# Attention feeding a SwiGLU block on one core: the first tiles' probabilities scaled by ScalarE and GpSimd ahead of plain transposes, and one threshold instruction for both heads

## The chip, the cores and the metric

The kernel runs on one core of one Trainium2 chip. The metric is the device time of one execution in microseconds (us), as the median over several executions. Five engines run their own instruction queues in order: PE (TensorE, matrix products and transposes), DVE (VectorE), ACT (ScalarE), POOL (GpSimd) and SP (SyncE, which here issues DMAs). An instruction starts when the one before it on its engine has been issued and the semaphores it waits for have arrived.

## The reference, cut to what matters

```python
# attention: q, k, v are (8, 8, 576, 64) float32
scores = scale * np.matmul(q, k.transpose(0, 1, 3, 2))
thresh = np.max(scores, axis=-1, keepdims=True) - tau
scores = np.where(scores >= thresh, scores, -1000000000.0)
scores = scores - np.max(scores, axis=-1, keepdims=True)
attn = np.exp(scores)
attn = attn / (np.sum(attn, axis=-1, keepdims=True) + 1e-09)
attn_out = np.matmul(attn, v)
# bridge: (B, H, S, D) -> x of (4608, 512); then, with weights that arrive as 64-bit floats
g = x @ w_gate
out = (g / (1 + np.exp(-g)) * (x @ w_val)) @ w_out
```

Each row of `scores` is cut at its own maximum minus `tau`, exponentiated, and divided by its own sum. What the change touches is how that division reaches the product with `v`, for a part of batch 0.

## The kernel before, in words

The batch is the outer loop. Batch 0 is handled by generators written out in an order by hand (`scores`, `flip_steps`, `attend_tile`, the `split_weights` family and `fill`). Batches 1 to 7 are handled by a planner (`Plan`), which orders jobs by cost; it is not touched by the change.

In batch 0 the heads are taken in four pairs, and a tile is 128 queries of one pair, so that two heads go through each step together. The first eight tiles are queries 0 to 255 of the four pairs, two tiles for each pair (`t < TA`, with `TA = 2`). The twelve tiles after them are the other queries of the same pairs (t = 2, 3 and 4; t = 4 has 64 queries, and its two heads share one tile of 128 rows). Here tiles are numbered in the order in which they run: 0 to 7 are the first eight, 8 to 19 the twelve after them.

One tile goes through these steps, with the line numbers of the kernel before:

- PE makes the scores of both heads into two PSUM tiles `sc` (L438). These PSUM tiles are two in number, so the scores of tile k+1 can start only when the masking of tile k has read them.
- DVE takes the negated row maximum `nm` of each head (L455).
- ACT computes the threshold `th` (L458) and the exponential into `p` (L459), for each head.
- DVE masks `p` against the threshold and sums its rows in the same instruction (L462). Two small instructions turn the sums into the reciprocal `ri` (L464, L465).
- The division. For tiles 8 and later, ACT multiplies the `p` of head 0 by `ri` (L472), and POOL does it for head 1 (L470). For tiles 0 to 7 `p` stays as it is, and ACT makes for each head a 128 x 128 diagonal matrix with `ri` on it (L478, from the identity).
- One tile later PE turns `p` round, so that keys lie on partitions: `flip_steps`. For tiles 8 and later these are transposes against the identity (L506); for tiles 0 to 7 they are matrix products of `p` with the diagonal (L508), which turn and divide at once. The 64 keys left over go through L512 or L514 into a bank `end`. ACT copies the results out of PSUM (L515, L522).
- One more tile later PE multiplies with `v` (L539, L541), and ACT copies the result into `x` (L544).

So while tile k is scored, tile k-1 is flipped and tile k-2 is attended: PE's order within tile k's slot is scores of k, product with `v` of k-2, flip of k-1.

Between these steps the same engines rebuild the FFN's weights, which come as 64-bit floats, one piece of 128 x 768 in each slot from tile 1 on. SP fetches a piece (L282), ACT splits it in two (L298, L299), POOL clamps the upper part (L291), one slot later DVE shifts it (L318), and one more later DVE joins the sign (L324) and POOL adds the lower part (L334). POOL also multiplies the queries by the softmax scale (L371) when their DMAs have landed.

The order on POOL matters. Within the first four segments (tiles 0 to 7) `early_slots[0]` is true, and `split_weights` issues the clamp at once, ahead of what the tile's generator issues next:

```python
            if n or x:
                split_weights()
                fetch_weights(2)
            next(go)
            clamp_split()
            add_lower(1)
```

Here `next(go)` runs the part of `scores` that holds L462 to L472. The scaling of the queries is called after it (`scales.popleft()()`), and the addition of the lower part belongs to `join_weights()` of the next slot. After tile 7 an extra attend of the tile just flipped comes, and then the first gate products (L555), before the scores of tile 9.

Of the kernel before, what the change touches and what calls it, by code (L numbers as in the profile page):

```python
# [13 lines left out]
AF = mybir.ActivationFunctionType  # L14
ALU = mybir.AluOpType
# [12 lines left out]
class Plan:  # L28
# [68 lines left out]
    def pe(self, took, fn, *deps):  # L97
        self.force(*deps)
        for d in deps:
            if d is not None:  # L100
                self.t = max(self.t, (d.end if isinstance(d, Job) else d) + self.HOP)
        self.run(self.t)
        fn()
        self.t += took
        return self.t + self.PIPE
# [7 lines left out]
def kernel(  # L113
# [11 lines left out]
    nc = tc.nc  # L125
    P = 128
# [21 lines left out]
    TA = 2  # L148
# [13 lines left out]
    cut = const.tile([P, 1], F32, name="cut")  # L162
# [48 lines left out]
    def room(n):  # L211
        nonlocal at
        at += n
        return pall[:, at - n:at]
# [3 lines left out]
    pbufs = deque(room(2 * S).rearrange("p (h s) -> p h s", h=2) for _ in range(2))  # L218
    ident = room(P)
    make_identity(nc, ident)  # L220
    dbufs = deque(room(2 * P).rearrange("p (h q) -> p h q", h=2) for _ in range(2))
    ones = room(TC)
    nc.vector.memset(ones, 1.0)
    pTbufs = deque(rall[:, 2 * x * S:2 * (x + 1) * S] for x in range(2))
# [198 lines left out]
    def turned(t):  # L423
        return TA <= t < NT

    def statistics(*names):
        return [stp.tile([P, 2 * NU3, 2] if x == "mx" else [P, 2 * NU3], F32, name=x) for x in names]

    def scores(seg, t):
        qT, kT = seg["qT"], seg["kT"]  # L430
        q0 = t * P - seg["q0"]
        if t < NT:
            pss = [ps_s.tile([P, 2, 512], F32, name="sc") for _ in range(2)]
            for h, hs in enumerate(heads):
                cut_ = D if turned(t) and h == 1 else 0
                for n, lo, to in [(0, 0, D), (0, D, SH), (1, 0, SH)] if cut_ else [(0, 0, SH), (1, 0, SH)]:
                    at_ = (n * SH + lo - cut_) % S
                    nc.tensor.matmul(pss[h][:, n, lo:to], qT[hs, q0:q0 + P], kT[hs, at_:at_ + to - lo],  # L438
                                     start=True, stop=True)
        else:  # L440
            pss = [ps_s.tile([P, 2, 512], F32, name="sc")]
            for n, h in ((0, 0), (1, 1), (1, 0), (0, 1)):
                hs = heads[h]
                nc.tensor.matmul(pss[0][hs, n, 0:SH], qT[hs, q0:q0 + D], kT[hs, n * SH:(n + 1) * SH],
                                 start=True, stop=True)
        nm, th, ri, tot = statistics("nm", "th", "ri", "tot")
        sm = sums[0]
        sums.rotate(1)
        m = len(pss)
        scs = [ps[:, :, 0:SH] for ps in pss]  # L450
        both = pbufs[0].rearrange("p h s -> p (h s)")[:, KM:KM + P]
        ps = [pbufs[0][:, x, :].rearrange("p (n s) -> p n s", n=2) for x in range(m)]
        pbufs.rotate(1)
        for x in range(m):
            nc.vector.tensor_reduce(out=nm[:, x:x + 1], in_=scs[x], axis=AX.XY, op=ALU.max, negate=True)  # L455
        yield
        for x in range(m):
            nc.scalar.activation(th[:, x:x + 1], nm[:, x:x + 1], AF.Identity, bias=cut, scale=-1.0)  # L458
            nc.scalar.activation(ps[x], scs[x], AF.Exp, bias=nm[:, x:x + 1])  # L459
        yield  # L460
        for x in range(m):
            nc.vector.scalar_tensor_tensor(out=ps[x], in0=scs[x], scalar=th[:, x:x + 1], in1=ps[x],  # L462
                                           op0=ALU.is_ge, op1=ALU.mult, accum_out=sm[:, x, 0:1])
        nc.vector.tensor_reduce(out=tot[:, 0:m], in_=sm[:, 0:m, 0:3:2], axis=AX.X, op=ALU.add)  # L464
        nc.vector.reciprocal(out=ri[:, 0:m], in_=tot[:, 0:m])  # L465
        units = [ident] * m
        if t >= TA:
            for x in range(m):
                if x % 2:
                    nc.gpsimd.tensor_scalar(out=ps[x], in0=ps[x], scalar1=ri[:, x:x + 1], scalar2=None, op0=ALU.mult)  # L470
                else:
                    nc.scalar.activation(ps[x], ps[x], AF.Copy, scale=ri[:, x:x + 1])  # L472
        yield
        if t < TA:
            units = [dbufs[0][:, x, :] for x in range(m)]
            dbufs.rotate(1)
            for x in range(m):
                nc.scalar.activation(units[x], ident, AF.Copy, scale=ri[:, x:x + 1])  # L478
        unflipped.append((seg, t, both, [(p.rearrange("p n s -> p (n s)"), unit) for p, unit in zip(ps, units)]))
        yield  # L480

# [44 lines left out]
    def attend_tile(copy=lambda xa, fn: (fn(), give_back(xa))):  # L526
        if not unattended:
            return
        if not xts:
            for u, lo in enumerate((0, 2 * XW)):  # L530
                xts["full", u] = xall[:, lo:lo + XW].rearrange("p (c n) -> p c n", c=NCC)
            xts["last", 0] = xlast
        seg, t, pT, pT2 = unattended.popleft()
        vr, vr2 = seg["v"]
        n = pT2.shape[1]
        xa = bank("xa")
        for kt in range(KT):
            for h in range(2):
                nc.tensor.matmul(xa[h * D:(h + 1) * D, 0:n], vr[:, h, kt, :], pT[:, h, kt, :],  # L539
                                 start=(kt == 0), stop=False)  # L540
        nc.tensor.matmul(xa[:, 0:n], vr2, pT2, start=False, stop=True)  # L541
        u, lo = divmod(t * P, TC)
        to = xts[("last", 0) if t == NT else ("full", u)][:, seg["i"], lo:lo + n]
        copy(xa, lambda: nc.scalar.copy(to, xa[:, 0:n]))  # L544
# [155 lines left out]
    for n, seg in enumerate(segs[:2 * NP]):  # L700
        early_slots[0] = n < NP
        if n >= NP:
            seg["v"] = segs[seg["i"]]["v"]
        for x, t in enumerate(seg["tiles"]):
            go = scores(seg, t)
            next(go)
            join_weights()
# [1246 lines left out]
    for s, (n, x) in enumerate((n, x) for n in range(len(halved)) for x in range(NU3)):  # L1954
        seg = halved[n]
        i, t = seg["i"], seg["tiles"][x]
# [11 lines left out]
        elif s == 1:  # L1968
            box = []
            m = pe(1.0, lambda: attend_tile(lambda *y: box.extend(y)))  # L1970
# [93 lines left out]
```

## Time and profile before

| | |
|---|---|
| time, median of 3 executions | 1373.08 us (1371.66 to 1374.05) |
| span of the profiled execution, first to last instruction | 1369.2 us |
| median less span | 3.88 us |
| the profiled execution's own time | not listed apart from its span |
| PE busy over the span | 1351.0 us (99%) |
| DVE, ACT, POOL busy over the span | 1070.9 (78%), 875.5 (64%), 719.9 (53%) us |
| granted TensorE clock | 1.000 over the span |
| tiles 0 to 7 (L508 products) | within the first 56 us |
| tiles 8 to 19 | about 50 to 130 us |

The page of a profile gives busy time per engine, the chain of work that ended last, and groups of instructions by source line. The timeline lists instructions in order: start, duration, engine, line, what is written and read, and in brackets the idle time of the engine just before it with what ended it. Consecutive like instructions are merged ("x16"), with one duration for all. An instruction's duration is longer than the distance to the next on the same engine where the two overlap.

### The profile page before, as it was taken

Reading aid. Unit: us, or ns where it says so; the run is one execution under the profiler, and the core shown is the slowest. Engines: PE = TensorE matmul, PEld = TensorE weight load, DVE = VectorE, ACT = ScalarE, POOL = GpSimd, SP = SyncE. Lnnn points to the kernel's source line nnn. Section 1 sums busy time; section 2 is a strip of 40 time slices with the busy share of each in tenths; the row PEclk is TensorE's granted clock in tenths of the full one; section 3 lists DMA queues with packets and bytes.
Section 4 is the critical chain, followed back from the end, with each engine's and each line's share of the span. In section 5 each row is a group of like instructions: output and inputs, shape, how many; then the busy total and the mean of one; then the engine's idle time right before and its main releaser. Section 6 shows DMA issues by size and latency. Waiting matters only on the chain.

```text
span 1369.2 us, 39187 instructions
## 1 busy us (share of the span) xinstructions
PE 1351.0 (99%) x15590; PEld 1116.1 (82%) x15590; DVE 1070.9 (78%) x2815; ACT 875.5 (64%) x2277; POOL 719.9 (53%) x665
## 2 busy tenths in 40 slices
PE   8999999999999999999999999999999999999998
PEld 7777787778788788877887888877887788999998
DVE  7878888887887777777778777777777776787786
ACT  6888776666756766677776766776767764330330
POOL 2688598663564669434973387427943593000000
PEclk9999999999999999999999999999999999999999
DMA  8752424545525540654154513553165403524411
GB/s 177 200 185 90 82 60 133 146 121 156 151 52 155 144 98 27 181 159 117 37 171 128 150 36 128 144 144 87 36 192 144 113 19 143 162 78 146 151 66 32
DMA packets 208294, 162.32 MB, mean 119 GB/s; under 512 B 166128, under 2 KB 180464, under 8 KB 202736
## 3 DMA queue, kind: packets, MB, share of 16 engines
q1 hardware_dynamic: 203920, 158.86, 41.3%
q8 instruction: 124, 2.03, 0.6%
q10 hardware_dynamic: 4192, 0.95, 0.3%
q14 instruction: 58, 0.48, 0.1%
HBM read 138.28 MB, written 21.50 MB: 117 GB/s over the span
## 4 chain that ended last, share of the span: by engine, by line
PE 90%; DVE 3%; DMA 2%; POOL 2%; SPq 1%; issue 1%; ACT 1%; ACTq 0%; DVEq 0%; POOLq 0%
PE pb L993 18%; PE pa L993 12%; PE px L1473 12%; PE sc L1705 10%; PE pe L993 9%; PE xa L1802 9%; PE po L1269 5%; PE py L1482 5%; PE sc L1154 2%; PE pg L1200 2%; PE pv L1200 2%; PE pe L1154 1%; SPq L367 1%; DMA wo<-in_moe_w_val_dram 1%; PE sc L1473 1%
## 5 line engine op out<-in xcount | busy, mean ns | idle before, releaser
L1753 DVE SCALAR_TENSOR_TENSOR pall<-sc,th,pall 128x288 f32<-128x288 f32 x504 | 244.0, 514 | 65.1 <-ACT pall L1751 50.7
L993 PE MATMUL pb<-xall,big 128*128 128x256 f32 x1152 | 273.5, 380 | 0.0
L1751 ACT ACTIVATE pall<-sc,nm 128x288 f32<-128x288 f32 x504 | 232.2, 498 | 34.1 <-DVE pall L1753 33.8
L993 PEld LDWEIGHTS pb<-xall,big 128*128 128x128 f32 x1152 | 216.4, 190 | 31.0 <-issue 2.2
L1781 DVE STREAM_TRANSPOSE pall<-pall 128x576 f32<-128x576 f32 x252 | 189.7, 765 | 58.2 <-ACT pall L1779 41.4
L1779 ACT ACTIVATE pall<-pall,ri 128x288 f32<-128x288 f32 x415 | 189.8, 529 | 26.3 <-DVE ri L1767 25.8
L846 POOL TENSOR_TENSOR hall<-hall,tmp 128x512 f32<-128x512 f32 x80 | 102.3, 1279 | 159.3 <-DVE hall L1046 141.9
L993 PE MATMUL pa<-xall,big 128*128 128x256 f32 x768 | 183.4, 382 | 0.0
L993 PEld LDWEIGHTS pa<-xall,big 128*128 128x128 f32 x768 | 143.0, 190 | 22.2 <-issue 2.7
L1705 PE MATMUL sc<-kT,qT 64*32 64x144 f32 (+1 forms) x5376 | 150.0, 345 | 2.9 <-DVE pall L1753 1.7
L1726 DVE TENSOR_REDUCE mx<-sc 128x2 f32<-128x576 f32 x168 | 124.8, 743 | 28.6 <-PE sc L1705 28.1
L1705 PEld LDWEIGHTS sc<-kT,qT 64*32 64x32 f32 x5376 | 97.8, 106 | 56.9 <-issue 21.0
L993 PE MATMUL pe<-xall,big 128*128 128x256 f32 x576 | 137.2, 381 | 0.4 <-issue 0.4
L1802 PE MATMUL xa<-pall,vall 64*32 64x288 f32 x4032 | 133.0, 404 | 0.9 <-DVE hall L1046 0.8
L1776 POOL TENSOR_SCALAR pall<-pall,ri 128x288 f32<-128x288 f32 x89 | 88.9, 1010 | 67.0 <-DVE ri L1767 63.8
L993 PEld LDWEIGHTS pe<-xall,big 128*128 128x128 f32 x576 | 108.5, 190 | 17.3 <-issue 2.8
L1802 PEld LDWEIGHTS xa<-pall,vall 64*32 64x32 f32 x4032 | 76.5, 107 | 50.6 <-issue 7.4
L1761 ACT COPY sums<-sums 32x6 f32<-32x6 f32 x336 | 66.8, 199 | 45.6 <-DVE pall L1753 41.1
L1045 ACT ACTIVATE vall<-tmp 128x512 f32<-128x512 f32 x96 | 60.2, 630 | 24.6 <-DVE tmp L1058 9.0
L1482 PE MATMUL py<-wo,hall 128*128 128x256 f32 x336 | 74.8, 379 | 0.0
L1728 DVE TENSOR_REDUCE mx<-sc 128x1 f32<-128x288 f32 x168 | 74.8, 445 | 0.0
L846 POOL TENSOR_TENSOR tmp<-tmp 128x512 f32<-128x512 f32 x36 | 45.9, 1276 | 53.4 <-ACT tmp L1068 53.4
(258 smaller groups left out, 2481.3 us busy)
## 6 DMA issues: line engine op xcount, KB each, us to landing
big<-sums_hbm SPq DMA_DIRECT2D x42, 1024.0 KB, 5.4
big<-sums_hbm SPq DMA_DIRECT2D x48, 768.0 KB, 4.7
vall<-in_v_dram SPq DMA_DIRECT2D x112, 144.0 KB, 3.0
out_dram<-big SPq DMA_DIRECT2D x32, 256.0 KB, 3.0
qT<-in_q_dram SPq DMA_DIRECT2D x112, 72.0 KB, 4.8
kT<-in_k_dram SPq DMA_DIRECT2D x112, 72.0 KB, 3.0
wo<-in_moe_w_gate_dram SPq DMA_DIRECT2D x16, 384.0 KB, 4.1
wo<-in_moe_w_val_dram SPq DMA_DIRECT2D x16, 384.0 KB, 4.8
```

The lines of the kernel that those rows point to most:

```text
L846: return lambda: nc.gpsimd.tensor_tensor(out=out, in0=a, in1=b, op=op)
L993: nc.tensor.matmul(ps[:, i], w[:, k_, i * P:(i + 1) * P], x[:, k_, :], start=first and i == k_ == 0, stop=True, skip_group_check=True)
L1473: nc.tensor.matmul(ps, a[:, f, :], ws[n][:, f, :], start=bank_ not in begun, stop=True, skip_group_check=True)
L1482: nc.tensor.matmul(ps(), a[:, f, i * P:(i + 1) * P], operands[o][:, f, :], start=first and f == 0, stop=True, skip_group_check=True)
L1705: nc.tensor.matmul(pss[h][(slice(g * G, (g + 1) * G), *part)], qT[hs, col:col + G], kT[hs, c * SH + keys[0]:c * SH + keys[1]], start=True, ...
L1726: rs.append(job("DVE", 0.72, lambda n=n, tile_=tile_: nc.vector.tensor_reduce(out=mx[:, n:n + 2, 0], in_=tile_[:, :, 0:SH], axis=AX.X, op= ...
L1751: ej = job("ACT", 0.42, lambda x=x, n=n: nc.scalar.activation(ps[x], scs[x], AF.Exp, bias=nm[:, n:n + 1]), ej, *((masks[h, 0], masks[h, 1] ...
L1753: masks[x] = job("DVE", 0.45, lambda x=x, n=n: nc.vector.scalar_tensor_tensor(out=ps[x], in0=scs[x], scalar=th[:, n:n + 1], in1=ps[x], op0 ...
L1776: scaled.append(job("POOL", 1.02, lambda x=x, n=n: nc.gpsimd.tensor_scalar(out=x, in0=x, scalar1=ri[:, n:n + 1], scalar2=None, op0=ALU.mul ...
L1779: scaled.append(job("ACT", 0.46, lambda x=x, n=n: nc.scalar.activation(x, x, AF.Copy, scale=ri[:, n:n + 1]), rj, rank=rank))
L1781: seg["turned"].append(job("DVE", 0.72, lambda both=both: nc.vector.transpose(out=both, in_=both), *scaled, rank=rank))
L1802: nc.tensor.matmul(holds[a].ap()[x * G:(x + 1) * G, 0:SH].rearrange("d (i q) -> d i q", q=G), vr[rs, h, j, ds], p[rs, h, :, j, :], start=( ...
```

## The change

Two things change in `scores`. The threshold is computed once for both heads (one instruction on 128 x 2 instead of two on 128 x 1), and it stands behind the exponential of head 0 instead of ahead of it; this holds for all twenty tiles of batch 0. For tiles 0 to 7 the diagonal matrices go, and `p` is multiplied by `ri` as in the later tiles: head 0 by ACT, head 1 by POOL. `flip_steps` is the same code, but its `unit` is now always the identity, so that tiles 0 to 7 take the branch of L506 (transposes) instead of L508. The products of the left-over keys (L512) stay, with the identity in place of the diagonal. The buffers of the diagonals are not allocated any more.

```diff
-    dbufs = deque(room(2 * P).rearrange("p (h q) -> p h q", h=2) for _ in range(2))
...
         for x in range(m):
-            nc.scalar.activation(th[:, x:x + 1], nm[:, x:x + 1], AF.Identity, bias=cut, scale=-1.0)
             nc.scalar.activation(ps[x], scs[x], AF.Exp, bias=nm[:, x:x + 1])
+            if x == 0:
+                nc.scalar.activation(th[:, 0:m], nm[:, 0:m], AF.Identity, bias=cut, scale=-1.0)
...
         units = [ident] * m
-        if t >= TA:
-            for x in range(m):
-                if x % 2:
-                    nc.gpsimd.tensor_scalar(out=ps[x], in0=ps[x], scalar1=ri[:, x:x + 1], scalar2=None, op0=ALU.mult)
-                else:
-                    nc.scalar.activation(ps[x], ps[x], AF.Copy, scale=ri[:, x:x + 1])
+        for x in range(m):
+            if x % 2:
+                nc.gpsimd.tensor_scalar(out=ps[x], in0=ps[x], scalar1=ri[:, x:x + 1], scalar2=None, op0=ALU.mult)
+            else:
+                nc.scalar.activation(ps[x], ps[x], AF.Copy, scale=ri[:, x:x + 1])
         yield
-        if t < TA:
-            units = [dbufs[0][:, x, :] for x in range(m)]
-            dbufs.rotate(1)
-            for x in range(m):
-                nc.scalar.activation(units[x], ident, AF.Copy, scale=ri[:, x:x + 1])
```

In the built order of the changed program, PE, DVE and SP hold the same instructions in the same order as before, apart from the transposes in place of the products. ACT's scaling of `p` stands where the two diagonals stood. On POOL, from tile 1 to tile 7, the new multiplication stands behind that tile's clamp, and ahead of the scaling of queries and of the addition of the next slot.

## The prediction

> **What bounds the stage now.** I read the page's chain first, then the busy time by stretches, then the chain of waits from 36 to 64 us, then the timeline from 8 to 90 us.
>
> ```profile
> PE 90%; DVE 3%; DMA 2%; POOL 2%; SPq 1%; issue 1%; ACT 1%; ACTq 0%; DVEq 0%; POOLq 0%
> ```
>
> Over the whole kernel PE sets the time, but the change lies in batch 0, and a stage has its own limits. The busy times by stretches (stretch, its length, then PE, PEld, DVE, ACT, POOL):
>
> ```profile
> 28.00:42.00 14.00, 12.84 (x115) 10.07 (x112) 13.39 (x26) 12.26 (x27) 10.84 (x9) 1.00 0.74 185
> 42.00:56.00 14.00, 13.48 (x116) 10.97 (x116) 12.47 (x27) 13.79 (x34) 10.85 (x8) 1.00 0.83 172
> ```
>
> ACT, DVE and PE are all nearly full, and POOL has some 3.2 us free in each 14. The chain of waits (start, length, what):
>
> ```profile
> 34.24 5.73 DMA wo<-in_moe_w_val_dram
> ...
> 41.86 0.30 ACT pall L478
> 42.16 0.04 issue
> 42.21 2.05 PE tp L508 x16
> ...
> 47.73 1.80 PE tp L508 x16
> ...
> 55.41 0.62 ACT big L515
> 56.03 0.04 issue
> 56.08 1.09 PE xa L539 x14
> 57.16 0.42 PE xa L541 x2
> 57.58 2.59 PE pg L555 x12
> 60.17 1.29 PE sc L438 x9
> ```
>
> A weight piece that lands at 39.97 resets the stage: ACT had stood idle 1.37 us for it. Then flips and ACT copies lead to the scores of tile 9 at 60.1 us. From there the chain goes on over DVE, POOL and PE with no DMA until 140, so I take a shift of tile 9's scores as a shift of the end, and 3.88 us (1373.08 - 1369.2) around the span as unchanged.
>
> **PE's part.** The flip of a tile was 16 rows of L508 in 1.95 us (at 24.64, 30.15); eight transposes L506 took 1.05 us (at 81.31). That removes 0.9 us a tile, 7.2 in eight tiles. What it is worth depends on who else is full.
>
> **ACT's part.** A threshold holds ACT 0.20 us (L458 at 9.57, the exponential at 9.77); one of two goes. The two diagonals held it 0.59 us (41.76 to the threshold at 42.35); the scaling of `p` holds it 0.66 us (L472 at 66.62, next at 67.28). Net -0.13 us a tile. ACT has 0.21 us idle in all from 41.76 to 53.5, so even with PE relieved this part alone gives about -0.13 x 3 = -0.4 us after the reset at 40.05, and PE's 0.9 goes into waiting for ACT. The new order of threshold and exponential costs nothing: before, the exponential ended 0.92 us after the threshold's start; now it ends at 0.72, and the threshold, from 0.62 on, takes 0.30 and ends at 0.92 too, which is when the masking can start. The wait for the second maximum (0.66 us later) lies under the exponential (0.72). In tiles 8 to 19 I take 0: masking there stands behind the second maximum and L324 on DVE.
>
> **POOL's part.** Eight multiplications of 1.87 us (L470 at 56.49, 65.79) are new, 15 us. Tiles 0 to 2 have room: POOL was idle 6.17, 3.52 and 4.57 us. Then, from the timeline:
>
> ```profile
> 28.75 0.93 POOL L371 TENSOR_SCALAR hall<-hall,scl 128x256 f32<-128x256 f32 x1 [4.57 <-DMA hall<-in_q_dram]
> 29.64 2.60 POOL L334 TENSOR_TENSOR big<-big,extra 128x768 uint32<-128x768 uint32 x1
> ...
> 30.15 1.95 PE L508 MATMUL tp<-pall 128*128 128x128 f32 x16
> ...
> 32.21 0.83 POOL L291 TENSOR_SCALAR big<-big 128x768 f32<-128x768 f32 x1
> 32.40 1.42 PE L438 MATMUL sc<-pall,qT 64*128 64x288 f32 x8
> 33.02 1.24 POOL L371 TENSOR_SCALAR hall<-hall,scl 128x320 f32<-128x320 f32 x1
> 34.23 1.81 POOL L334 TENSOR_TENSOR big<-big 128x768 uint32<-128x768 uint32 x1
> ```
>
> POOL waits for queries until 28.75, adds, and clamps tile 3's piece at 32.21. None of that moves, since SP's train of DMA issues is the same. The multiplication for tile 3 is queued behind this clamp, though `ri` of tile 3 was there at 27.9. Its flip, which ran from 30.15, now waits. Queued behind the flip on PE are its left-over products and the scores of tile 5; on ACT, the copies out of PSUM, and behind these tile 4's split, scaling and tile 5's exponential. Step by step (hops of 0.04 us):
>
> - Tile 3. Multiplication 33.04 + 1.87 = 34.9. Four transposes hold PE 0.5, the left-over products 0.37: scores of tile 5 at 35.8 (before 32.40, +3.4). ACT's last copies end about 36.2, so tile 4's L298 starts there (before 32.83, +3.4).
> - Tile 4. POOL: 34.9 + L371 1.08 + L334 1.81 = 37.8, clamp 0.83 = 38.6, multiplication 1.87 = 40.5. Transposes and copies 1.4: tile 5's L298 at 41.9 to 42.4 (before 40.05, +1.9 to +2.3; the upper value where L324 at 38.4 holds POOL's start back 0.5). The 1.37 us for which ACT used to wait for its DMA has paid for the difference.
> - Tile 5. A new ring: L298 0.93, clamp 0.83, multiplication 1.87, four transposes to their end 0.66, copy 0.59, last copy's start 0.16, five hops 0.2: 5.24 us. L298 stood 5.18 apart before (40.05 to 45.23). Hence tile 6's L298 stays +2.0 to +2.4.
> - Tiles 6 and 7. POOL itself paces: L371 1.08 + L334 1.81 + clamp 0.83 + multiplication 1.87 = 5.6 us against 5.2 a tile before: +0.4, and +0.3 more where a shift on DVE and POOL's long instructions shut each other out. Tile 7's L298 (before 50.42) and then its second copy L515 (before 56.02) stand +2.4 to +3.1.
>
> Behind that copy follow product with `v`, gate products and tile 9's scores, as the chain shows: 60.1 becomes 62.5 to 63.2. POOL has 4.15 us idle before 63.75, so its backlog ends there. The sum is +2.8 us, taken in the upper half because the shutting-out is seen in this trace: 1373.08 + 2.8 = 1375.9 us.
>
> **The unknown: POOL's multiplication against DVE.** Rows (timeline):
>
> ```profile
> 65.79 1.88 POOL L470 TENSOR_SCALAR pall<-pall,ri 128x576 f32<-128x576 f32 x1 [0.22 <-DVE ri L465]
> 67.06 0.94 DVE L324 SCALAR_TENSOR_TENSOR big<-wo,big 128x768 uint32<-128x768 uint32 x1
> 84.59 1.84 POOL L334 TENSOR_TENSOR big<-big 128x768 uint32<-128x768 uint32 x1
> 85.41 1.43 DVE L318 TENSOR_SCALAR big<-big 128x768 uint32<-128x768 uint32 x1
> ```
>
> A shift L318 that met an addition L334 took 1.43 instead of 0.54 us: it was kept out until L334's end. But L324 started within a multiplication L470 and took its ordinary 0.94. So between this multiplication and DVE I take 0. The dear bound: half an L470 (0.9 us) lost once in each of tiles 5 to 7, another +2.8. The cheap bound: no shutting-out at all, POOL's 5.6 against 5.2 alone, some +1.3 in all.
>
> The Trainium skill, page "SBUF — State Buffer", section "SBUF: two separate sides", says that a GpSimd instruction and a VectorE instruction in a two-port mode or with two SBUF inputs lock each other out for the whole instruction. L318 behind L334 agrees (1.43 us); L324 under L470 does not (0.94 us). By the rule in full the sum would be the dear one, 1378.7 us.
>
> **Rivals.**
> - Faster, by PE: the chain names the flips of tiles 5 and 6, and tile 7's is like them. If the chain is taken at its word, 3 x 0.9 + 3 x 0.2 (thresholds) = -3.3, 1369.8 us. It needs POOL's multiplication of tile 3 done by about 31 us, when head 0's transposes are over, and ACT not full. Against it: the clamp ahead of it ended at 33.04, and ACT's 13.79 of 14 us. Chance 0.09.
> - Caught up: POOL's idle times from 28 to 66 sum to 10.85 us (0.90, 1.51, 0.87, 0.34, 1.21, 0.34, 0.89, 0.42, 4.15, 0.22) and five multiplications need 9.4, so that the stall could be made good, down to +1: 1374.1 us. Against it: the largest of them ends only at 63.75, after the scores of tile 9. Chance 0.12.
> - Dearer, by the lock: 1378.7 us, from the point where L318 or L324 on DVE is stretched under L470. Chance 0.14.
> - That it doesn't do what it says: the built order shows it does; no chance of its own.
>
> **How the numbers follow.** My forecast has the other 0.65. 0.2% is 2.75 us, about what a measurement of this kernel can tell from no change, and +2.8 lies on that edge: of 0.65, 0.36 is beyond it and 0.29 within. Slower 0.36 + 0.14 = 0.50; same 0.29 + 0.12 = 0.41; faster 0.09. The range goes from 1373.3 (just under the cheap bound's +1.3, and the caught-up case) to 1379.0 (the dear bound).
>
> **What would show it.** Right: GpSimd's multiplication for tile 3 at 33.0 to 33.2; PE idle some 3.5 us before the second head's transposes, released by POOL; scores of tile 5 at 35.8, of tile 9 at 62.5 to 63.2; flips of about 1.05 us in busy time; ACT no longer idle for the weight piece at 40. Wrong: tile 9's scores at or before 60.1; L318 or L324 at 1.8 us and more under a multiplication of tiles 3 to 7 (the lock); or a shift at tile 9 that is gone by 140.

## The result, and the profile after

| | before | changed |
|---|---|---|
| time, median (nine executions of each, side by side) | 1372.97 us (1370.48 to 1374.77) | 1375.39 us (1374.28 to 1377.37) |
| ratio changed / before | | 1.0020, 95% interval 1.0012 to 1.0029 |
| span of the profiled execution | 1369.2 us | 1374.0 us |
| its own time | not listed | 1376.13 us (2.13 around the span) |
| its mean granted clock | 1.000 | 0.996 |
| PE, DVE, ACT, POOL busy | 1351.0, 1070.9, 875.5, 719.9 us | 1348.5, 1072.2, 872.7, 731.2 us |

The changed kernel is 1.6 to 4.0 us slower. PE has 2.5 us less to do and POOL 11.3 more, and the span is still 4.8 us longer. In the changed kernel these lines stand 1 lower than before (L371 is now L370, L334 L333, L291 L290, L298 L297, L318 L317, L324 L323, L438 L437); the multiplication on POOL is L469, ACT's scaling L471, the transposes L500.

The page's chain of work of the changed kernel hardly differs from the one before, which shows how little a chain over 1374 us can tell about a stage:

```profile
PE 90%; DVE 3%; POOL 2%; DMA 2%; SPq 1%; issue 1%; ACT 1%; ACTq 0%; DVEq 0%; POOLq 0%
```

The busy times by stretches (PE, PEld, DVE, ACT, POOL; then the granted clock) do show it:

```profile
28.00:42.00 14.00, 9.08 (x67) 6.22 (x66) 8.89 (x17) 8.71 (x18) 11.38 (x9) 0.76 0.74 188
42.00:56.00 14.00, 12.67 (x103) 9.11 (x104) 13.79 (x29) 13.66 (x27) 13.58 (x10) 1.00 0.85 194
```

From 28 to 42 us all engines but POOL lost work (PE 12.84 to 9.08, DVE 13.39 to 8.89, ACT 12.26 to 8.71): something made them all wait. And the granted clock is 0.76, where it was 1.00. In the next stretch POOL has gone from 10.85 to 13.58 of 14 us and is full. The timeline (start, duration, engine, line, what; in brackets the idle time before it and what ended it) names the wait:

```profile
29.57 1.60 POOL L370 TENSOR_SCALAR hall<-hall,scl 128x256 f32<-128x256 f32 x1 [3.99 <-DVE nm L454]
31.14 1.80 POOL L333 TENSOR_TENSOR big<-big,extra 128x768 uint32<-128x768 uint32 x1
32.91 0.82 POOL L290 TENSOR_SCALAR big<-big 128x768 f32<-128x768 f32 x1
33.71 1.72 POOL L469 TENSOR_SCALAR pall<-pall,ri 128x576 f32<-128x576 f32 x1
35.48 1.12 PE L500 MATMUL tp<-pall 128*128 128x128 f32 x4 [4.92 <-POOL pall L469]
36.53 0.70 PE L506 MATMUL end<-pall 128*64 128x128 f32 x4
37.16 2.30 PE L437 MATMUL sc<-pall,qT 64*128 64x288 f32 x8
...
63.66 1.36 PE L437 MATMUL sc<-pall 64*128 64x288 f32 x10
```

Query scaling, addition, clamp, and only then tile 3's multiplication; PE stands still for 4.92 us ahead of the second head's transposes. When it resumes, its rows are long: four transposes take 1.12 us (0.66 in the tiles around), eight rows of scores 2.30 (1.42 before). Tile 5's scores start at 37.16 (before 32.40, +4.8), tile 9's at 63.66 (before 60.10, +3.6).

The shift does not stay what it is at tile 9. The table follows PE's scores through the planner's part, from the timelines of both kernels:

| start of the scores, before | 60.10 | 130.69 | 142.23 | 153.06 | 165.68 | 184.78 | 353.82 | 664.46 | 1130.63 |
|---|---|---|---|---|---|---|---|---|---|
| changed, later by | 3.56 | 3.35 | 3.36 | 5.83 | 7.46 | 6.97 | 6.25 | 4.86 | 4.74 |

There is a second place, near 150. The chains of waits of the two kernels there (start, length, what), before and after:

```profile
140.08 6.43 DMA extra<-in_moe_w_out_dram
...
146.54 0.93 ACT wo L873
...
153.06 2.13 PE sc L1705 x50
```

```profile
144.62 7.75 DMA extra<-in_moe_w_out_dram
...
152.40 0.91 ACT wo L867
...
158.89 3.47 PE sc L1699 x50
```

A piece of `w_out` is issued 4.54 us later (3.35 of it is the shift; the four key DMAs ahead of it on SP took 4.40 us to issue instead of 3.29) and takes 7.75 us to land instead of 6.43. ACT waits for it with the maxima, the threshold and the exponentials of the next scores queued behind. PE then stands idle 3.64 us instead of 1.17, and again its rows come out long (3.47 for 2.13). Of the 7.0 us reached by 185, some 2.2 are won back between 340 and 655. PE's short gaps there in the kernel before (0.37 us at 344.35, 0.47 at 640.86) are missing in the changed one, which accounts for under half of it; the rest I have not traced.

Both places end with PE at half clock (stretch, length, PE busy first, granted clock third from the end):

```profile
33.40:39.90 6.50, 4.42 (x22) 2.73 (x24) 2.52 (x4) 3.09 (x5) 6.12 (x6) 0.50 0.79 226
...
159.60:162.90 3.30, 3.30 (x64) 2.39 (x49) 2.50 (x6) 2.23 (x7) 2.97 (x3) 0.50 0.04 10
```

Half of 4.42 and of 3.30 us of PE work is 3.9 us of lengthening, against 4.8 us of longer span. Knock-on delays elsewhere aside, that is an upper bound for what the clock itself costs, since some of these rows would have been waited for anyway.

### The profile page after: what moved, and what is told of

Its sections match the earlier page's. It is cut to its first block, busy times and chain, and to the rows that moved or that the text cites. A ratio compares the mean times of both kernels' runs of the same rounds, so it can differ in the third digit from the quotient of the medians.

```text
span 1374.0 us, 39044 instructions
## 1 busy us (share of the span) xinstructions
PE 1348.5 (98%) x15526; PEld 1108.1 (81%) x15526; DVE 1072.2 (78%) x2815; ACT 872.7 (64%) x2253; POOL 731.2 (53%) x673
## 4 chain that ended last, share of the span: by engine, by line
PE 90%; DVE 3%; POOL 2%; DMA 2%; SPq 1%; issue 1%; ACT 1%; ACTq 0%; DVEq 0%; POOLq 0%
PE pb L987 18%; PE pa L987 12%; PE px L1467 12%; PE sc L1699 10%; PE pe L987 9%; PE xa L1796 9%; PE po L1263 5%; PE py L1476 5%; PE sc L1148 2%; PE pg L1194 2%; PE pv L1194 2%; PE pe L1148 1%; SPq L366 1%; POOL pall L469 1%; POOL big L333 1%
```

## The experiments

All of them were timed beside the kernel before, and ratios are to it. Theory A: the loss is one stall, tile 3's multiplication late in POOL's queue (A2: without it the stall moves to tile 4). Theory B: POOL has too much to do in every slot of tiles 4 to 7. Theory C, the clock theory: PE's idle time costs more than its length, since PE runs at half clock after it. Rivals: the threshold, VectorE held out, PE's work itself.

### Which part of the change

**threshold_alone**: the kernel before with the merged threshold only.

```diff
         for x in range(m):
-            nc.scalar.activation(th[:, x:x + 1], nm[:, x:x + 1], AF.Identity, bias=cut, scale=-1.0)
             nc.scalar.activation(ps[x], scs[x], AF.Exp, bias=nm[:, x:x + 1])
+            if x == 0:
+                nc.scalar.activation(th[:, 0:m], nm[:, 0:m], AF.Identity, bias=cut, scale=-1.0)
```

> The kernel before with only the threshold merged and put behind head 0's exponential; diagonals and their products stay. My theory (the loss comes from the multiplication's place in GpSimd's queue) expects no loss here: ACT is held 0.2 us less for each of tiles 5 to 7, so -0.4 us to 0 against the kernel before, with the scores of tile 5 at 32.4 us as before. A rival, that the new order of threshold and exponential delays the masking, expects +0.2 us or more a tile, +1 to +3 us.

Measured: 1370.9 us, ratio 0.9996 (0.9984 to 1.0008). The threshold is worth nothing that these runs can show. But its profiled execution held a surprise. It has no multiplication of the first tiles on POOL, and yet (timeline, then stretches):

```profile
39.21 2.99 PE L438 MATMUL sc<-pall,qT 64*128 64x288 f32 x8 [1.97 <-DVE pall L463]
```

```profile
39.80:46.40 6.60, 6.60 (x34) 5.19 (x33) 5.63 (x14) 4.07 (x8) 4.12 (x4) 0.50 0.89 236
```

PE waited 1.97 us for the masking of tile 5, then worked 6.6 us without a gap at a clock of 0.50; tile 9's scores came at 62.75 instead of 60.10. So the structure of before falls to half clock too, in some of its executions. In that execution the queries had landed late (L371 on POOL at 29.71, before 28.75).

**scaling_alone**: the change with the two separate thresholds put back (the diff above, reversed, on the changed kernel).

> The changed kernel with the two thresholds put back as they were: only the scaling of p ahead of plain transposes. My theory expects the whole loss here: +2 to +4 us against the kernel before, and PE idle near 30 to 35 us until GpSimd's multiplication for tile 3 ends. The rival of the threshold expects the loss to shrink to under +1 us.

Measured: 1374.52 us, ratio 1.0023 (1.0012 to 1.0034): the whole loss. Tile 3's multiplication stood at 32.98, PE idle 4.29 us behind it, transposes 1.12, scores of tile 5 at 36.82 in 2.30 us, tile 9 at 63.63.

### Where in the queue

**queries_later**: the change, with the query scaling that waits for its DMA issued one slot later, so that tile 3's multiplication no longer stands behind it.

```diff
-            if n == 0 and x == 1 or n == 1:
+            if n == 0 and x == 1:
+                scales.popleft()()
+            elif n == 1 and x == 1:
+                scales.popleft()()
                 scales.popleft()()
```

> The changed kernel with one move on GpSimd: the scaling of the queries of pair 3, which waits for its DMA until about 29 us, is issued one slot later, behind tile 3's multiplication. All work stays. Theory A (the loss is one stall: tile 3's multiplication queued behind that wait) expects tile 3's multiplication at 28.9 us or so instead of 33.7, no stall of PE near 30 us, the weight piece near 40 us waited for again, and -2.5 to -3.5 us against the change, that is -0.5 to +0.5 against the kernel before. Theory B (GpSimd has too much to do in every slot of tiles 4 to 7, 5.6 us against 5.2) expects the scores of tile 9 still 1.3 us or more late and a time +1 to +2.5 against the kernel before.

Measured: 1372.5 us, ratio 1.0007 (0.9995 to 1.0018). Tile 3's multiplication moved to 29.06, and tile 5's scores to 31.80. Scaling_alone was timed in the same series: by the ratios (0.0007 against 0.0023) the one reordering leaves about a third of its loss, by the medians (1.75 of 3.77 us) nearly half. Tile 9's scores came at 61.60, 1.5 us late, as theory B expected; theory A alone expected no loss. What is left is the next tile's turn (timeline; DVE, POOL, PE):

```profile
35.28 1.46 DVE L323 SCALAR_TENSOR_TENSOR big<-wo,big 128x768 uint32<-128x768 uint32 x1
...
35.90 2.42 POOL L469 TENSOR_SCALAR pall<-pall,ri 128x576 f32<-128x576 f32 x1
...
38.38 1.12 PE L500 MATMUL tp<-pall 128*128 128x128 f32 x4 [2.81 <-POOL pall L469]
...
40.05 2.30 PE L437 MATMUL sc<-pall,qT 64*128 64x288 f32 x8
```

Tile 4's multiplication stands behind an addition and a clamp, meets L323 on DVE and takes 2.42 us instead of 1.72 (L323 1.46 instead of 0.95). PE waits 2.81 us, and then runs its scores in 2.30 us again.

**tile3_on_act**: the change, with head 1 of tile 3 scaled by ACT.

```diff
-            if x % 2:
+            if x % 2 and (seg["i"], t) != (1, 1):
```

> The changed kernel, but tile 3's multiplication of head 1 is done by ACT instead of GpSimd; the other seven stay on GpSimd. Theory A (one stall at tile 3) expects the time of the kernel before, -0.5 to +0.5 us. In the run with the queries scaled later, tile 3's stall went, but the next one came at tile 4 (its multiplication at 35.90, 2.42 us long, PE idle 2.8 us) and about a third of the loss was left. Theory A2 (GpSimd is late from tile 3 on, and taking one long instruction out of its way only moves the stall to tile 4) expects PE to wait for GpSimd at tile 4's flip, 1 to 3 us, and +0.7 to +2 us against the kernel before.

Measured: 1373.11 us, ratio 1.0011 (1.0002 to 1.0020). PE's waits for POOL from 28 to 64 us (us in total, times, longest):

```profile
PE tp L500 <- POOL pall L469: 4.3, 3, 3.0
```

Three microseconds of wait are now tile 4's (at 39.11). The stall moves from tile 3 to tile 4 rather than going away: POOL's backlog is one of a queue, not of one instruction.

**all_on_act**: in tiles 0 to 7 ACT scales both heads.

```diff
-            if x % 2:
+            if x % 2 and t >= TA:
```

> The changed kernel with all multiplications of tiles 0 to 7 on ACT, none on GpSimd. Theory A2 (GpSimd's queue) expects no wait of PE for GpSimd in these tiles; ACT is held 0.66 - 0.13 = 0.5 us a tile longer than before, which is hidden up to the weight piece at 40 us and costs 3 x 0.5 = 1.5 us from tile 5 to tile 7, so +1 to +2 us against the kernel before, less than the change's +3. If the loss had nothing to do with GpSimd, the time would stay at the change's or above, +3 to +5.

Measured: 1372.78 us, ratio 1.0011 (1.0001 to 1.0020). No wait for POOL is left; tile 9's scores at 61.44. ACT has two scalings in each tile instead of one, and PE waits for DVE and ACT in its place. ACT is busy for all of the 14 us from 28 to 42, and again from 42 to 56, and POOL was busy for 13.58 of the latter 14 in the changed kernel: neither engine has room for this work in tiles 3 to 7.

### What the clock does

These kernels add products of constants on PE, by a helper that the kernel already has for its first microseconds (`run_idle`); their results are not read.

```python
    def run_idle(n):
        ps = bank("idle")
        for _ in range(n):
            nc.tensor.matmul(ps[:, 0:TC], ones[:, 0:P], ones, start=True, stop=True)
        give_back(ps)
```

**pe_filled** (20 products), **pe_filled_half** (10), **pe_filled_seven** (7): between the two heads' transposes of tile 3.

```diff
         for h, (p, unit) in enumerate(ps):
+            if h == 1 and (seg["i"], t, seg["q0"]) == (1, 1, 0):
+                run_idle(20)
```

> The changed kernel with 20 unused products on PE between the two heads' transposes of tile 3, so that PE does not stand idle while it waits for GpSimd there; nothing uses their result. In the changed kernel the granted clock fell to 0.66 in the stretch from 36 to 42 us, after PE's 4.9 us of waiting, and the four transposes there took 1.12 us instead of 0.66, the scores 2.30 instead of 1.42. If that slow clock carries part of the loss (theory C), the clock stays at 1.0, scores of tile 5 end about 1.4 us earlier, and the time is -0.7 to -1.5 us against the change. If the stall alone counts, the tile 9 scores move by under 0.3 us and the time stays.

> As the run with PE filled, with 10 unused products (20 rows of about 0.22 us, 4.4 us) instead of 20, so that they end before GpSimd's multiplication does. In the changed kernel the granted clock was 0.50 from 33.6 to 40.8 us. Theory C (the slow clock carries part of the loss) expects 1.0 throughout, the same start of tile 3's second transposes (35.4 us), tile 5's scores done 1.4 us earlier, and -1 to -2 us against the change (+1.5 to +2.5 against the kernel before). If only the stall counts, the time is that of the change within 0.5 us.

> The change with 7 unused products between the two heads' transposes of tile 3 (14 rows; ten took 4.48 us in the run before, so 3.1 us here). Where the transposes of head 0 end at 30.4, these products end at 33.5, ahead of the multiplication of tile 3 (to 35.4), so that nothing useful waits for them, and PE's longest idle time becomes 2.0 instead of 4.9 us. Clock theory: the granted clock stays at 1.00, the second head's transposes take 0.66 us instead of 1.12 and the scores of tile 5 1.42 instead of 2.30, the scores of tile 9 come at 61.5 to 62.5 instead of 63.66, and the time lies 1 to 2 us under that of the change: a ratio of 1.0005 to 1.0015. Rival (the late multiplication and POOL's and ACT's pace set it all, the clock only lengthens work that PE would wait for anyway): the scores of tile 9 stay at 63.3 to 63.7, ratio 1.002 to 1.0025.

Measured: 1377.31 us, 1.0035 (1.0022 to 1.0048); 1374.29 us, 1.0029 (1.0016 to 1.0041); 1373.73 us, 1.0019 (1.0008 to 1.0030). The first was sized wrong: a product is two rows, 20 took 8.80 us and ended at 39.2, long after the multiplication. The clock was 1.00 and the scores of tile 5 took 1.25 us, but they started at 39.92. The second's profiled execution had fallen to half clock already at tile 2 (its scores 2.99 us at 16.43), so that its products started 2 us late. (The second expectation puts the half clock of the changed kernel at 33.6 to 40.8; its trace has 33.2 to 40.0.) Both are inconclusive on theory C. The third fits in time, and its profile is the telling one (timeline, then stretches):

```profile
35.50 0.65 PE L502 MATMUL tp<-pall 128*128 128x128 f32 x4 [1.91 <-POOL pall L469]
...
36.45 2.20 PE L437 MATMUL sc<-pall,qT 64*128 64x288 f32 x8
```

```profile
36.70:40.00 3.30, 3.30 (x22) 2.29 (x22) 1.33 (x2) 3.17 (x6) 3.30 (x3) 0.50 0.97 358
```

The transposes after the wait ran at full clock, 0.65 us; a microsecond after PE had resumed, the clock fell to 0.50 for 3.4 us, in the middle of full work. My expectation that 1.9 us of idle time would leave the clock alone failed. Tile 9's scores came at 62.97, between what the two theories said; the ratio, 1.0019, is next to the rival's 1.0020.

**queries_later_filled**: queries_later, with 5 products ahead of the second head's transposes of tile 4 (`== (2, 0, 0)`, `run_idle(5)`).

> The kernel of the run with the query scaling one slot later, and 5 unused products (some 2.3 us) between the two heads' transposes of tile 4, where PE stood idle from 35.6 to 38.4. Clock theory: the granted clock stays at 1.00 through 36 to 42 (it was 0.62 there), the scores of tile 6 take 1.42 instead of 2.30 us, tile 9's come at 60.3 to 61 instead of 61.60, and the time is 1370.5 to 1371.5, a ratio of 0.9990 to 1.0000: nothing of the loss is left. Rival (what is left of the loss in that run is POOL's pace and the wait for the multiplication of tile 4): tile 9's scores at 61.4 or later, ratio 1.0005 to 1.001.

Measured: 1371.53 us, ratio 1.0008 (0.9993 to 1.0023), by twelve executions from 1370.64 to 1379.14, so the ratio cannot tell. In the profiled one the clock held 1.00 through 36 to 42, tile 6's scores took 1.25 us and tile 9's came at 60.64 (61.60 without the products). Its five executions at a mean clock of 1.000 took 1370.92 to 1371.60 us, about 1 us more than the kernel before at that clock (median 1370.16, ten executions of the same series). Expected was nothing: about 1 us is left. POOL's pace and the products themselves are the likely reasons; no run parts them.

**before_filled**: the kernel before, with 5 products ahead of the scores of tile 6.

```diff
+            if n == 3 and x == 0:
+                run_idle(5)
```

> The kernel before, with 5 unused products on PE ahead of the scores of tile 6, where PE stands idle 1.1 to 2 us (it waits for the masking of tile 5); nothing uses their result. In 32 executions of the kernel before, the 15 with a mean granted clock of 1.000 had a median of 1369.6 us, the 10 with 0.996 to 0.998 took 1371.9 to 1375.9. If that spread is PE's clock falling after this idle time, the clock is 1.000 in nearly all executions, the median falls to 1369.3 to 1370 and the spread narrows. If the clock only shows what late transfers do, the spread and the median (1370.8) stay.

Measured: 1370.76 us, ratio 0.9994 (0.9985 to 1.0003). All twelve executions lie at a clock of 0.999 or 1.000 and within 1369.83 to 1372.32 us; the kernel before, beside it, ranged from 1369.40 to 1375.28. The median did not reach the 1369.3 to 1370 expected, and its gain is within the interval; the narrower spread is plain.

The executions of the kernel before point the same way without any edit. Sorted by the mean clock that each was granted (110 executions in four series):

| mean granted clock | 1.000 | 0.999 | 0.998 | 0.997 | 0.996 |
|---|---|---|---|---|---|
| first series, median us (executions) | 1369.63 (15) | 1371.14 (7) | 1373.17 (3) | 1373.55 (4) | 1374.69 (3) |
| second series | 1370.02 (13) | 1371.46 (8) | 1373.19 (8) | 1373.70 (4) | 1375.24 (2) |
| third series | 1370.16 (10) | 1371.69 (6) | 1371.89 (6) | 1373.30 (5) | 1375.70 (2) |
| fourth series | 1370.77 (7) | 1370.45 (4) | 1371.14 (1) | 1373.64 (1) | 1374.79 (1) |

All nine executions of the changed kernel were at 0.995 to 0.997, and none of scaling_alone's twelve was above 0.998. The table is a correlation: a longer wait both lowers the clock and costs time by itself.

Which waits bring half clock is not settled. In the clock records of the traces every stretch between two changes is a whole number of steps of 3.413 us (27.31, 6.83, 119.47 and 3.41 us in the changed kernel: 8, 2, 35 and 1 steps). So the clock changes only at the ends of equal steps, and these lie differently in each execution: the first rise to 1.00 came 4.5 to 7.2 us after the first instruction. The length of a wait sorts most cases. Of the eleven waits of PE of 1.9 us or more in these profiles nine were followed by a fall, and none of those of 1.1 to 1.9 us was. But three rows do not fit (timeline; pe_filled, pe_filled_half, first_three):

```profile
159.93 2.13 PE L1701 MATMUL sc<-kT,qT 64*32 64x288 f32 x64 [2.67 <-DVE pall L1749]
...
16.43 2.99 PE L437 MATMUL sc<-pall,qT 64*128 64x288 f32 x8 [0.86 <-DVE pall L462]
...
117.77 2.06 PE L438 MATMUL sc<-pall 64*128 64x288 f32 x10 [0.89 <-DVE pall L463]
```

After the first wait (and one of 2.68 us in pe_filled_seven) the clock stayed at 1.00; around the other two it fell to 0.50, at 16.9 and at 119.9, with no longer wait before it. So one profiled execution at full clock, like that of queries_later_filled, does not show that the products held it up. The stronger evidence is the count: all 24 executions of before_filled and threshold_filled (below) were at 0.999 or 1.000, beside 37 of 64 of the kernel before in the same two series.

### A version that beats both

**threshold_filled**: before_filled with the merged threshold.

> The kernel before with the merged threshold alone, and the 5 unused products ahead of the scores of tile 6. If the 0.2 us that the merged threshold saves ACT in each tile reaches the path once the clock stays up, the ratio falls under that of the kernel with the unused products alone (0.9994): to 0.9985 to 0.9990, that is 0.6 us for tiles 5 to 7 on top, and beats both kernels. If ACT's relief is swallowed by other waits, 0.9990 to 0.9998, as without it.

Measured: 1370.18 us (1369.12 to 1371.61), ratio 0.9988 (0.9978 to 0.9997), all twelve at a clock of 0.999 or 1.000. It is faster than the kernel before by 0.4 to 3.0 us, where the change is slower; the interval ends close to 1, and this is the best of twelve variants timed. At a clock of 1.000 the kernel before takes 1370.16 us in the same series, so the gain can be put down to half clock that no longer happens. What the merged threshold adds is not shown: tile 9's scores came at 59.38 (59.88 in before_filled), but the intervals of the two ratios overlap.

**first_three**: the same, with the scaling of `p` in tiles 0 to 2 alone, where POOL has idle time.

```diff
+        plain = t >= TA or (seg["i"], t) in ((0, 0), (0, 1), (1, 0))
-        if t >= TA:
+        if plain:
```

> The kernel of the run threshold_filled, with the scaling of p by ScalarE and GpSimd in tiles 0 to 2 alone; tiles 3 to 7 keep the diagonals. Theory (the loss begins with tile 3, whose multiplication is queued behind GpSimd's late clamp; tiles 0 to 2 have idle time on GpSimd, and what PE saves there is taken back at the weight piece that lands at 40): no wait of PE for GpSimd over 0.5 us, scores of tile 5 at 31.8 to 32.5, of tile 9 within 0.5 us of threshold_filled's, ratio 0.998 to 0.9995. Rival (any of these multiplications costs, for instance by holding VectorE or ScalarE, wherever it stands): tile 9's scores 1 us or more later, ratio 1.0000 or above.

Measured: 1371.03 us, ratio 1.0002 (0.9992 to 1.0012); tile 9's scores at 60.28, 0.9 us later than in threshold_filled. It gains nothing, the expectation of 0.998 to 0.9995 failed, and where the 0.9 us comes from is not settled: the rival, that these multiplications cost something even where POOL has idle time, is not excluded. Seven of its eleven executions were at 0.999 or 1.000; the profiled one fell to half clock at 119.9, far behind the products. Tile 1's multiplication pushes the query scaling behind it from 18.78 to 20.39, and the next queries were scaled at 29.96 instead of 28.82; but that time varies from 28.75 (before) to 30.38 (all_on_act) over these profiles, and threshold_alone, without a multiplication there, had 29.71.

## Why the prediction was right, and where it was not

The forecast was 1375.9 us with slower by over 0.2% and no change at nearly even chances; it came to 1375.39 us, +0.2%. The mechanism is the one predicted: tile 3's multiplication queued behind GpSimd's late clamp, PE standing idle with the release by POOL, the loss carried to tile 9 and on. That the sum came out close is partly luck: two errors in it cancelled.

- **The new order of the threshold: no cost.** Borne out as far as the runs can tell (0.9996, interval on both sides of 1).
- **Flips.** Eight transposes take 1.04 us (at 41.03); 1.05 was read off.
- **Tile 3.** Multiplication predicted at 33.0 to 33.2, found at 33.71 (32.98 in scaling_alone). The step "none of that moves" failed by 0.8 us: the query scaling before it began at 29.57, not 28.75. SP's eight query issues ahead of it took 5.88 us instead of 5.19, and that start varies between executions. The multiplication itself took 1.72 us, not 1.87.
- **PE's idle time.** 4.92 us instead of some 3.5: 0.5 from the later release, and 0.9 because head 0's transposes ended at 30.56, sooner than I had put them.
- **Scores of tile 5.** 37.16 instead of 35.8: the later release, and 0.7 us for transposes and left-over products at half clock, which the prediction did not know of.
- **Tiles 4 to 7.** L297 of tile 5 at 43.04 (predicted 41.9 to 42.4), and ACT no longer waits there for the weight piece, as said. Then 5.07 us to tile 6 (predicted 5.24) and 5.64 to tile 7 (5.6 from POOL's pace, 5.9 with shutting-out). Tile 9's scores at 63.66, half a microsecond past the range of 62.5 to 63.2. Here the working holds; what it started from was late.
- **The lock.** Zero was nearly right for the join behind a multiplication that already ran, and not for the shift; the shifts lost time to additions as predicted (timeline):

```profile
33.77 1.09 DVE L317 TENSOR_SCALAR big<-big 128x768 uint32<-128x768 uint32 x1 [1.31 <-POOL big L290]
...
44.89 1.72 POOL L469 TENSOR_SCALAR pall<-pall,ri 128x576 f32<-128x576 f32 x1
45.34 1.10 DVE L323 SCALAR_TENSOR_TENSOR big<-wo,big 128x768 uint32<-128x768 uint32 x1
47.64 1.82 POOL L333 TENSOR_TENSOR big<-big,extra 128x768 uint32<-128x768 uint32 x1
48.29 1.60 DVE L317 TENSOR_SCALAR big<-big 128x768 uint32<-128x768 uint32 x1
```

  Tile 3's shift started 0.06 us behind its multiplication (33.71) and took 1.09 us (0.54 alone); in scaling_alone the same meeting left the shift at 0.56 and the multiplication took 2.12 instead. L323, started within a multiplication, took 1.10 us (0.95 alone) and ended before it. L317 within an addition took 1.60 (0.54 alone), and ended about 0.4 us after it. In queries_later, where the multiplication came second, it took 2.42 us. The dear rival's condition (L317 or L323 at 1.8 us under a multiplication) was not met in the changed kernel. The rule weighed there, that either side shuts the other out for its whole instruction, fits the shift against the addition and the multiplication that comes second, and neither the shift nor the join that starts within a multiplication: both ended before it.
- **"A shift of tile 9's scores is a shift of the end."** Wrong in both directions: 3.35 at 131, 7.0 at 185, 4.7 at 1131. The view of 36 to 64 us could not show that a weight piece of the planner's part is issued behind the shift and sets ACT back once more.
- **The half clock.** The step that failed most, by omission: nothing in the profile shown, of an execution at a clock of 1.000, pointed to it. Against that profile the change costs 4.8 us, not 2.8.
- **What cancelled it.** I put 3.88 us around the span and took that as unchanged. Executions listed with their spans have 2.1 to 2.3; the profiled one of before, at full clock, took by that some 1371.3 us (1369.2 + 2.13). The median of before (1373.08) very likely holds half-clock stretches already, which the change could not add again: no clock is listed for its executions, but in the later series all of the kernel before over 1373 us were at 0.996 to 0.998. Profile to profile +4.8, median to median +2.4.
- **The range.** Its lower end, 1373.3, is put "just under" the cheap bound and the caught-up case, but lies 1.1 and 0.8 us under them (1374.4 and 1374.1).

How the loss divides is known by a rough estimate only. At full clock the reordered kernel was about 1 us slower than before, and the one execution of pe_filled_seven at 1.000 took 1372.41 us, 2.3 more than before at that clock. So of the 4.8 us some 1 to 2.5 are waiting by itself, by estimate from these, and the rest goes with half clock; no kernel held the clock up in the changed order without adding waits of its own.

The Trainium skill, page "TensorE: Matmul & The Clock Gate", section "What's actually happening", says that the gate passes either half or all of the clock pulses, and judges by free-running windows of about 3.4 us. The rows here agree on the levels (0.50 and 1.00) and on the length: 36.6 to 40.0 in pe_filled_seven, 159.5 to 162.9 in the changed kernel, twice that (39.7 to 46.5) in threshold_alone. The steps of 3.413 us in the clock records agree with such windows. The same page, section "Why this matters for your kernels", advises to keep PE's idle gaps under about 3 us; here half clock followed waits of 1.97 and 1.91 us, and even of 0.86 and 0.89, and it did not follow waits of 1.17, 1.67 and 2.67 us (before at 153, all_on_act at 40, pe_filled at 160).

## What to carry to other kernels

Before moving work to an engine with a low share of busy time, write out its queue where the new instruction would stand: what counts is when the instruction ahead of it ends, here a clamp behind a wait for a DMA, and idle time elsewhere does not help. A new wait of about 2 us or more on TensorE may cost more than its length, since 3.4 or 6.8 us at half clock can follow it after PE has resumed. Here it followed nine of eleven such waits. Five unused products in a known gap kept the clock up here, and with the merged threshold beside them the kernel beat the one before. And look at how the executions of the kernel before spread by granted clock, before the span of one of them is compared with a median of many.

## What the runs showed of the hardware

- After a wait of PE of 1.91 us (pe_filled_seven) and of 1.97 us (threshold_alone) the granted clock fell to 0.50 about 1 us after PE had resumed (at 36.6, with work from 35.50) or half a microsecond after (39.7, with work from 39.21). It stayed there for 3.4 or 6.8 us although PE was busy throughout. In the changed kernel, with 4.92 us of waiting, it fell within the wait (at 33.2) and stayed low to 40.0.
- In every profile the granted clock, from its first rise on, changed only after whole steps of 3.413 us. Nine of eleven waits of PE of 1.9 us or more were followed by half clock, and two of the eleven falls came with no wait above 0.9 us.
- The same program, unchanged, ran from 1368.4 to 1375.9 us in 110 executions, and its medians rise nearly throughout as its mean granted clock falls from 1.000 to 0.996.
- A GpSimd multiplication by a per-partition factor (128 x 576, float32) took 1.72 us in the first tiles and 1.87 later, and 2.42 when VectorE's join was running as it was to start (queries_later). Started first, it left the join at 1.10 us, and a shift at 1.09 instead of 0.54 (changed kernel).
